# An identity matrix from VectorE and one small matmul, and GpSimd's constants in another order

## The chip, the cores and the metric

The kernel runs on one core of one Trainium2 chip. The metric is the device time in microseconds (us) of one execution. Its work is spread over the core's engines: TensorE (PE, with its weight loads shown apart as PEld), VectorE (DVE), ScalarE (ACT), GpSimd (POOL) and SyncE (SP), which here only issues DMAs. Each engine runs its own instructions in a fixed order; between engines they wait on semaphores that count finished instructions.

## What is computed

A parallel transformer block over 2048 positions of width 512: a layer norm, then a dilated local attention with 32 heads of 16 (8 keys for each query, two positions apart) and a gated GELU network of width 1376, both added to the input.

```python
x = A_x
xn = _layernorm(x, axis=-1)
return x + _A_ref(xn, A_wqkv, A_wo) + _B_ref(xn, B_w_gate, B_w_up, B_w_down)
```

In `_A_ref` the logits are dot products over 16 features with the keys at distances 0, 2, ... 14; positions before the start are masked; softmax over the 8 keys, a weighted sum of values, and a projection by `wo`. In `_B_ref` it is `gelu(xn @ w_gate) * (xn @ w_up) @ w_down`.

## The kernel before

The 2048 positions are cut into 4 blocks of 512, each into 4 tiles of 128; a pair of tiles (256 positions) is loaded as one `XIN` buffer. The program builds a graph of named tasks, one instruction or a run of matmuls each, and the table `ORDER` states by hand, engine by engine, the order in which the tasks are issued. From the graph come the semaphore waits; nothing is reordered at run time.

**The start.** SP loads the first tiles of x. PE meanwhile runs dummy matmuls on a constant of ones (`warm0` to `warm14`, L637): nine of 512 columns and one of 128 ahead of the first transposes, five of 128 behind them. DVE and ACT normalise tile 0 (`bnst0` L717, `bnag0` L743, `sub0` L828, `sq0` on ACT L753, `rstd0` L806, `norm0a/b` L847). PE transposes the first tiles against the identity `ident` (`tpx`, `tpy`, L888 and L877, four matmuls for each pair). From the transposed `xnT` it makes Q, K and V.

**The constants.** GpSimd makes, in this order: ones in `cf`, `onef` (for ACT's first table load), the identity by a selection on `cf` (L600) and a copy to bf16 (`c_idb`, L603), zeros in front of V (L618), `eps`, `mhalf`; then `E8`, a 128x32 matrix with 4 entries in each column that sums products over groups of 4 partitions: a fill (L607), two selections (L608, L611) and a copy to fp16 (L614); zeros in front of K (L616); the mask of the first positions, a fill (L622) and a selection (L623); zeros in `UT` (L621). DVE's first task is `c_wdz` (L620), zeros in a corner of `Wd`. A selection (`affine_select`) keeps or replaces each element by its place; each reads and writes SBUF. `cf`, `E8f` and `mask` are edited in place, so their steps wait for each other.

**Block 0's attention.** ACT copies the four Q tiles of block 0 out of PSUM (`evq0_0` to `evq0_3`, L988). DVE then multiplies Q by the 8 shifted views of K in two large `tensor_tensor` instructions of 8192 elements on each partition (`pr0_0`, `pr0_1`, L1066) and adds the halves (`pa0`, L1078). PE sums the products with `E8` (`er0_3`: 16 matmuls at L1102 for another purpose, then 16 with `E8` at L1109). DVE adds the mask once (L1132); ACT copies the logits out (`lc0`, L1138); the softmax goes on in short DVE steps that start with the maximum (L1143). DVE's queue around it reads `norm4 pr0_0 pr0_1 pa0 rstd8 h0_1 h0_0 mask d1a_0`, the h tasks being the products of the gated network (L1279).

**The later norms.** For tiles 8 to 15 the statistics come from ACT, which would need a table switch for a square root; GpSimd takes it instead as a power of one half over two columns (`sq8`, `sq10`, `sq12`, `sq14`, L799). `ve8` on ACT (L795) hands the variance to `sq8`; `rstd8` on DVE (L770) inverts it, and `norm8` on ACT (L820) uses it, with block 0's `gelu0_5` and `lc0` queued behind it.

GpSimd's queue and DVE's first task in `ORDER`, and the order in which a task is made to follow another of another engine:

```python
"pool":
    "c_ones c_onef c_id c_vnpad c_idb c_eps c_mhalf c_e8a c_e8b c_e8c c_e8d c_ktpad c_mask0 c_mask1 c_utz "
    "sq8 sq10 sq12 sq14",

def order_after(t, pred):
    if pred is not t and pred not in t.deps:
        t.deps.add(pred)
        t.odeps.add(pred)
```

Of the kernel before, what the change touches and what calls it, by code (L numbers as in the profile page):

```python
# [96 lines left out]
class Graph:  # L97
# [251 lines left out]
    def report(self):  # L349
# [4 lines left out]
BF = mybir.dt.bfloat16  # L354
F32 = mybir.dt.float32
FP16 = mybir.dt.float16
ALU = mybir.AluOpType
# [5 lines left out]

ORDER = {
# [34 lines left out]
    "dve":  # L399
# [10 lines left out]
    "pool":  # L410
        "c_ones c_onef c_id c_vnpad c_idb c_eps c_mhalf c_e8a c_e8b c_e8c c_e8d c_ktpad c_mask0 c_mask1 c_utz "
# [28 lines left out]
def bass_parallel_sum__sliding_local_dilated__glu_gated_geglu__prompt_kernel(nc, A_x, A_wqkv, A_wo, B_x, B_w_gate, B_w_up, B_w_down, out, dbg=None, cfg=None):  # L440
# [27 lines left out]
    QSC = 2.0 ** -6  # L468
# [15 lines left out]
    with contextlib.ExitStack() as es:  # L484
        def sb(name, shape, dt):
            return es.enter_context(nc.sbuf_tensor(name, shape, dt))
# [5 lines left out]
        Wd = sb("Wd", [128, NJ, 512], BF)  # L492
# [1 line left out]
        xnT = sb("xnT", [128, NXT, 4, 512], BF)  # L494
        KT = sb("KT", [128, 2, 4, 528], BF)
        ident = sb("ident", [128, 128], BF)
        cf = sb("cf", [128, 128], F32)
        E8 = sb("E8", [128, 32], FP16)
        E8f = sb("E8f", [128, 32], F32)
        mask = sb("mask", [32, 2, 4, 16], F32)  # L500
        one_l = nc.const_aps.tensor(1.0, [128, 128], BF)
        one_r = nc.const_aps.tensor(1.0, [128, 512], BF)
# [33 lines left out]
        PS = es.enter_context(nc.psum_tensor("PS", [128, 4096], F32))  # L536
# [7 lines left out]
        G = Graph()  # L544
        P_ps = Pool("ps", 8, psum=True, quotas=QUOTAS)
# [22 lines left out]
        I_wd = Item("Wd")  # L568
        I_wo = Item("Wo")
        I_ident = Item("ident")  # L570
        I_cf = Item("cf")
        I_E8 = Item("E8")
        I_E8f = Item("E8f")
# [21 lines left out]
        PC = -1000  # L595
        I_htz = Item("htz")
        PC2 = cfg.get("PC2", 8)
        G.task("pool", "c_ones", 0.2, lambda e: e.memset(cf[:, :], 1.0), wr=[I_cf], prio=PC)
        G.task("pool", "c_onef", 0.1, lambda e: e.memset(onef[:, :], 1.0), wr=[I_onef], prio=PC)
        G.task("pool", "c_id", 0.3, lambda e: e.affine_select(  # L600
            out=cf[:, :], in_=cf[:, :], pattern=[[-1, 128]], compare_op=ALU.is_equal, fill=0.0, base=0,
            channel_multiplier=1), rd=[I_cf], wr=[I_cf], prio=PC)
        G.task("pool", "c_idb", 0.65, lambda e: e.tensor_copy(out=ident[:, :], in_=cf[:, :]),  # L603
               rd=[I_cf], wr=[I_ident], prio=PC)
        G.task("pool", "c_mhalf", 0.1, lambda e: e.memset(mhalf[:, :], 0.5), wr=[I_mhalf], prio=PC2)
        G.task("pool", "c_eps", 0.1, lambda e: e.memset(eps[:, :], 1e-5), wr=[I_eps], prio=PC)
        G.task("pool", "c_e8a", 0.1, lambda e: e.memset(E8f[:, :], 0.25 / QSC), wr=[I_E8f], prio=PC2)  # L607
        G.task("pool", "c_e8b", 0.25, lambda e: e.affine_select(  # L608
            out=E8f[:, :], in_=E8f[:, :], pattern=[[-4, 32]], compare_op=ALU.is_ge, fill=0.0, base=0,
            channel_multiplier=1), rd=[I_E8f], wr=[I_E8f], prio=PC2)  # L610
        G.task("pool", "c_e8c", 0.25, lambda e: e.affine_select(  # L611
            out=E8f[:, :], in_=E8f[:, :], pattern=[[4, 32]], compare_op=ALU.is_ge, fill=0.0, base=3,
            channel_multiplier=-1), rd=[I_E8f], wr=[I_E8f], prio=PC2)
        G.task("pool", "c_e8d", 0.25, lambda e: e.tensor_copy(out=E8[:, :], in_=E8f[:, :]),  # L614
               rd=[I_E8f], wr=[I_E8], prio=PC2)
        G.task("pool", "c_ktpad", 0.15, lambda e: e.memset(KT[:, KTI[0].slot, :, 0:16], 0.0), wr=[(KTI[0], "pad")],  # L616
               prio=PC2)
        G.task("pool", "c_vnpad", 0.15, lambda e: e.memset(VN[:, VNI[0].slot, :, 0:16], 0.0), wr=[(VNI[0], "pad")],  # L618
               prio=PC2)
        G.task("dve", "c_wdz", 0.25, lambda e: e.memset(Wd[0:32, 10, :], 0.0), wr=[(I_wd, 2)], prio=PC + 1)  # L620
        G.task("pool", "c_utz", 0.6, lambda e: e.memset(UT[0:32, :], 0.0), wr=[I_htz], prio=PC2 + 20)  # L621
        G.task("pool", "c_mask0", 0.2, lambda e: e.memset(mask[:, :, :, :], 0.0), wr=[I_mask], prio=PC2)  # L622
        G.task("pool", "c_mask1", 0.3, lambda e: e.affine_select(  # L623
            out=mask[:, :, :, :], in_=mask[:, :, :, :], pattern=[[8, 2], [2, 4], [1, 16]],
            compare_op=ALU.is_ge, fill=-1.0e9, base=-14, channel_multiplier=0),
            rd=[I_mask], wr=[I_mask], prio=PC2 + 10)
        G.task("act", "c_tbl", 1.3, lambda e: e.activation(
            out=onef[:, 1:2], in_=onef[:, 0:1], func=ACTF.Sqrt),
            rd=[(I_onef, 0)], wr=[(I_onef, 1)], prio=PC, table="sqrt")
# [14 lines left out]
        for i, nm in enumerate(("q", "k", "v")):  # L644
            def mk(i=i):
# [4 lines left out]
                         prio=(-958, -957.5, -898)[i], nbytes=(900 if i == 0 else 512) * 1024)  # L650
# [10 lines left out]
        for (i, src, c0, c1, o) in ((0, B_w_gate, 1280, 1376, 32), (1, B_w_up, 1280, 1312, 0),  # L661
                                    (2, B_w_up, 1312, 1376, 128)):
            def mk(src=src, c0=c0, c1=c1, o=o):
# [8 lines left out]
            wr=[(I_wd, 0)], prio=R_WD, nbytes=2000 * 1024)  # L672
# [5 lines left out]
                     wr=[I_wo], prio=R_WD + 2, nbytes=512 * 1024)  # L678
# [9 lines left out]
        for p in range(NP):  # L688
            b = p // 2
            base = LN_BASE[b] + (p % 2) * 10  # L690
# [3 lines left out]
            if p < 2:  # L694
                for t2 in range(2):
                    def mk_ld(t2=t2, p=p, it=it_x):
# [3 lines left out]
                                 prio=((-960, -959), (-957.8, -956.5))[p][t2], nbytes=128 * 1024)  # L700
            else:
                def mk_ld(p=p, it=it_x):
# [3 lines left out]
                             prio=(0, 0, -897.5, -897)[p] if p < 4 else -950 + p * 20, nbytes=256 * 1024)  # L706
# [6 lines left out]
            for t2 in range(2):  # L713
                t = 2 * p + t2
# [3 lines left out]
                if t == 1:  # L718
                    for (nm, dur, kw, rd, wr) in (
# [6 lines left out]
                        def mk_a(kw=kw, it=it_x):  # L726
                            return lambda e: e.activation(**dict(dict(in_=XIN[:, it.slot, 1, :]), **kw))
                        t_of[nm] = G.task("act", nm, dur, mk_a(), rd=rd + ([] if "in_" in kw else xp(it_x, p, 1)),
                                          wr=wr, prio=-300)
                    t_of["mean1"] = G.task("dve", "mean1", 0.1, lambda e: e.tensor_scalar(  # L730
                        out=mv[:, 1, 0:1], in0=sums[:, 0:1], scalar1=1.0 / D, scalar2=None, op0=ALU.mult),
                        rd=[(I_sums, 0)], wr=[(I_mv, 1)], prio=tp0(t))
# [12 lines left out]
            for ts in (((2 * p,), (2 * p + 1,)) if b == 0 else ((2 * p, 2 * p + 1),)):  # L745
                t, n = ts[0], len(ts)
# [8 lines left out]
                if t < NSQA:  # L755
                    t_of["sq%d" % t] = G.task("act", "sq%d" % t, 0.15, mk_sa(), rd=[(I_sums, 2) if t == 1 else (I_mv, t), I_eps],
                                              wr=[(I_sq, t)], prio=pr - 100, table="sqrt")
                else:
# [12 lines left out]
                    if p < PACT:  # L771
                        t_of["sq%d" % t] = G.task(
                            "act", "sq%d" % t, 0.25, lambda e, t=t, n=n: e.activation(
                                out=sq[:, t:t + n], in_=mv[:, t:t + n, 1], func=ACTF.Sqrt, bias=eps[:, 0:1]),
                            rd=[(I_mv, q) for q in ts] + [I_eps], wr=[(I_sq, q) for q in ts], table="sqrt")
# [4 lines left out]
                    for t2 in range(2):  # L780
                        def mk_sqa(t=t + t2, t2=t2, it=it_x):
# [3 lines left out]
                               wr=[I_xs, (I_s2, t + t2)], prio=pr + 2)  # L785
                    small("act", "va", [I_s2], I_vb, scale(vb, s2, 1.0 / D))
                    if p < PPOW:
                        t_of["sq%d" % t] = G.task(
                            "act", "sq%d" % t, 0.25, lambda e, t=t, n=n: e.activation(
                                out=sq[:, t:t + n], in_=vb[:, t:t + n], func=ACTF.Sqrt, bias=eps[:, 0:1]),  # L790
                            rd=[(I_vb, q) for q in ts] + [I_eps], wr=[(I_sq, q) for q in ts], table="sqrt")
# [4 lines left out]
                            out=ve[:, t:t + n], in_=vb[:, t:t + n], func=ACTF.Identity, bias=eps[:, 0:1]),  # L796
                        rd=[(I_vb, q) for q in ts] + [I_eps], wr=[(I_ve, q) for q in ts])
# [11 lines left out]
            for t2 in range(2):  # L809
                t = 2 * p + t2  # L810
# [591 lines left out]
        for b in range(NB):  # L1402
            for j in range(NJ - 1):
                G.order_after(t_of["fu%d_%d" % (b, j)], t_of["fg%d_%d" % (b, j)])
                if j >= 4:
                    G.order_after(t_of["fg%d_%d" % (b, j)], t_of["fu%d_%d" % (b, j - 4)])
                if j >= 1:
                    G.order_after(t_of["fg%d_%d" % (b, j)], t_of["fg%d_%d" % (b, j - 1)])
                    G.order_after(t_of["fu%d_%d" % (b, j)], t_of["fu%d_%d" % (b, j - 1)])
        G.schedule(ORDER)  # L1410
        G.assign_sync(cnt, dsems)
        REPORT.update(G.report())
# [32 lines left out]
```

## Time and profile before

| what | value |
|---|---|
| time, median of 3 runs (lowest to highest) | 181.36 us (181.31 to 181.4) |
| time of the profiled execution | 181.5 us |
| span of its instructions | 180.0 us |
| mean traffic of the DMAs | 109 GB/s |
| HBM read and written | 14.71 MB, 3.15 MB |

The span runs from the first instruction of the program in the trace to the last; the 1.5 us between it and the time of the same execution lie around it. Rows of the timeline read: start in us from the span's begin, duration in us, engine, line of the kernel, operation, what it writes and reads, shape, count of merged instructions, and in brackets the engine's idle time before it with what ended it. The duration of one row of several instructions runs from the first start to the last end.

### The profile page before, as it was taken

The numbers are of one execution on the slowest core, as the hardware profiler recorded it, in microseconds if no ns is written. First come the engines' busy times: TensorE is split into PE (matmuls) and PEld (weight loads), VectorE is DVE, ScalarE is ACT, GpSimd is POOL, SyncE is SP. The second block draws the span as 40 slices with busy tenths as digits, with TensorE's granted clock in tenths as the row PEclk, the third lists the DMA queues.
The fourth block names the chain that finished last, engine by engine and source line by source line (L and its number), as shares of the span: only waits on it lengthen the run. The fifth ranks groups of instructions, "written<-read, shape, count | busy, mean of one in ns | idle before, by whom it ended". The sixth has DMA issues, their size and how long they took to land.

```text
span 180.0 us, 2755 instructions
## 1 busy us (share of the span) xinstructions
PE 176.1 (98%) x1043; PEld 91.7 (51%) x1060; DVE 168.8 (94%) x157; ACT 132.9 (74%) x270; POOL 20.0 (11%) x23
## 2 busy tenths in 40 slices
PE   8999999999999999999999999999999999999995
PEld 2897554444544445444444454444444444446555
DVE  3899998799999999999999999999999999999973
ACT  5689999999999998999895798953276676611111
POOL 6000160000720009207000000000000000000000
PEclk9999999999999999999999999999999999999999
DMA  4995690863260400002744000243060226810023
GB/s 125 362 357 152 121 324 13 293 224 98 58 227 18 98 4 0 0 0 60 193 129 88 29 0 0 77 123 124 18 217 4 58 58 192 272 60 4 0 73 102
DMA packets 27276, 19.60 MB, mean 109 GB/s; under 512 B 13856, under 2 KB 25088, under 8 KB 27264
## 3 DMA queue, kind: packets, MB, share of 16 engines
q1 hardware_dynamic: 27264, 19.44, 36.5%
q8 instruction: 8, 0.13, 0.3%
q14 instruction: 4, 0.03, 0.1%
HBM read 14.71 MB, written 3.15 MB: 99 GB/s over the span
## 4 chain that ended last, share of the span: by engine, by line
PE 96%; ACT 2%; issue 1%; DVE 0%
PE PS L1255 38%; PE PS L1347 29%; PE PS L1035 17%; PE PS L952 3%; PE PS L637 3%; PE PS L1010 2%; PE PS L1294 2%; PE PS L966 1%; PE PS L1102 1%; ACT UU L1272 1%; PE PS L1109 0%; PE PS L888 0%; ACT XS L736 0%; ACT XIN L820 0%; ACT OB L1380 0%
## 5 line engine op out<-in xcount | busy, mean ns | idle before, releaser
L1347 PE MATMUL PS<-Wd,HT 128*128 128x512 bf16 (+2 forms) x206 | 40.2, 345 | 0.2
L1255 PE MATMUL PS<-xnT,Wu 128*128 128x512 bf16 x158 | 39.0, 379 | 0.2 <-ACT UU L1272 0.2
L1255 PE MATMUL PS<-xnT,Wg 128*128 128x512 bf16 x155 | 38.4, 379 | 0.4 <-issue 0.2
L1217 DVE TENSOR_TENSOR UNI<-VN,PT 128x8192 f16<-128x8192 bf16 x8 | 35.2, 4416 | 0.0
L1066 DVE TENSOR_TENSOR UNI<-QT,KT 128x8192 f16<-128x8192 bf16 x8 | 35.2, 4417 | 0.0
L1035 PE MATMUL PS<-xnT,Wqkv 128*128 128x512 bf16 x140 | 34.0, 379 | 0.3 <-ACT XS L736 0.2
L1347 PEld LDWEIGHTS PS<-Wd,HT 128*128 128x128 bf16 x209 | 19.6, 98 | 19.0
L1380 ACT ACTIVATE OB<-PS 128x512 bf16<-128x512 f32 x14 | 8.3, 594 | 24.0 <-PE PS L1347 22.5
L1272 ACT ACTIVATE UU<-PS 128x512 bf16<-128x512 f32 x40 | 23.4, 605 | 3.0 <-PE PS L1255 1.5
L1265 ACT ACTIVATE GG<-PS 128x512 bf16<-128x512 f32 x40 | 23.2, 599 | 3.2 <-PE PS L1255 2.7
L1255 PEld LDWEIGHTS PS<-xnT,Wu 128*128 128x128 bf16 x160 | 15.5, 98 | 18.9 <-ACT GG L1265 0.4
L1255 PEld LDWEIGHTS PS<-xnT,Wg 128*128 128x128 bf16 x160 | 15.6, 98 | 18.5 <-ACT UU L1272 0.4
L799 POOL TENSOR_TENSOR sq<-ve,mhalf 128x2 bf16<-128x2 f32 x4 | 17.1, 4280 | 64.3 <-ACT ve L795 64.3
L1035 PEld LDWEIGHTS PS<-xnT,Wqkv 128*128 128x128 bf16 x144 | 16.2, 113 | 15.3 <-ACT GG L1265 0.4
L1078 DVE TENSOR_TENSOR UNI<-UNI 128x8192 f16<-128x8192 f16 x4 | 17.7, 4418 | 0.1
L1226 DVE TENSOR_TENSOR UNI<-UNI 128x8192 f16<-128x8192 f16 x4 | 17.7, 4419 | 0.0
L1347 PE MATMUL PS<-Wo,OT 128*128 128x512 bf16 (+2 forms) x74 | 16.0, 345 | 0.1
L1279 DVE TENSOR_TENSOR HT<-GG,UU 128x1024 bf16<-128x1024 bf16 x20 | 13.2, 684 | 0.4 <-ACT UU L1272 0.4
L1347 PEld LDWEIGHTS PS<-Wo,OT 128*128 128x128 bf16 x76 | 7.1, 98 | 6.5 <-DVE OT L1237 0.2
L1232 DVE TENSOR_TENSOR UNI<-UNI 128x4096 f16<-128x4096 f16 x4 | 9.1, 2287 | 0.1
L1046 ACT ACTIVATE VN<-PS 128x512 bf16<-128x512 f32 x12 | 7.1, 601 | 2.0 <-PE PS L1035 1.9
L1046 ACT ACTIVATE KT<-PS 128x512 bf16<-128x512 f32 x12 | 7.1, 602 | 1.6 <-PE PS L1035 1.5
(98 smaller groups left out, 181.1 us busy)
## 6 DMA issues: line engine op xcount, KB each, us to landing
PT<-pt_scratch SPq DMA_DIRECT2D x16, 256.0 KB, 4.0
out_dram<-OB SPq DMA_DIRECT2D x14, 128.0 KB, 2.1
XIN<-in_A_x_dram SPq DMA_DIRECT2D x12, 128.0 KB, 3.9
Wqkv<-in_A_wqkv_dram SPq DMA_DIRECT2D x3, 512.0 KB, 5.0
XIN<-in_A_x_dram SPq DMA_DIRECT2D x6, 256.0 KB, 5.3
Wg<-in_B_w_gate_dram SPq DMA_DIRECT2D x2, 640.0 KB, 6.6
Wu<-in_B_w_up_dram SPq DMA_DIRECT2D x2, 640.0 KB, 6.6
Wd<-in_B_w_down_dram SPq DMA_DIRECT2D x1, 1280.0 KB, 6.5
```

Of the source, the lines that this page charges most:

```text
L799: "pool", "sq%d" % t, 5.0, lambda e, t=t, n=n: e.tensor_tensor(out=sq[:, t:t + n], in0=ve[:, t:t + n], in1=mhalf[:, 0:n], op=ALU.pow),
L1035: ins = e.matmul(PS[:, 512 * it.slot:512 * it.slot + 512], lhsT=wcols(which, kt, g), rhs=xnT[:, itx.slot, kt, :], start=(kt == 0), stop=(k ...
L1046: return e.activation(out=o, in_=PS[:, 512 * it.slot:512 * it.slot + 512], func=ACTF.Identity, scale=(QSC, 1.0, 1.0)[which])
L1066: return lambda e: e.tensor_tensor(out=UNI[:, it.slot:it.slot + 2, :, :], in0=bass.AP(QT, (itq.slot * 4 + 2 * h) * 512, [[NQT * 4 * 512, 1 ...
L1078: return lambda e: e.tensor_tensor(out=UNI[:, i0.slot:i0.slot + 2, :, :], in0=UNI[:, i0.slot:i0.slot + 2, :, :], in1=UNI[:, i1.slot:i1.slo ...
L1217: return lambda e: e.tensor_tensor(out=bass.AP(UNI, ito.slot * 4096, [[NUNI * 4096, 128], [2048, 4], [512, 4], [1, 512]]), in0=bass.AP(VN, ...
L1226: return lambda e: e.tensor_tensor(out=UNI[:, i0.slot:i0.slot + 2, :, :], in0=UNI[:, i0.slot:i0.slot + 2, :, :], in1=UNI[:, i1.slot:i1.slo ...
L1255: ins = e.matmul(PS[0:M, 512 * it.slot:512 * it.slot + 512], lhsT=Wx[:, kt, j * 128:j * 128 + M], rhs=xnT[:, itx.slot, kt, :], start=(kt = ...
L1265: return lambda e: e.activation(out=GG[:, ito.slot, q, :], in_=PS[:, 512 * it.slot:512 * it.slot + 512], func=ACTF.Gelu_apprx_tanh)
L1272: return lambda e: e.activation(out=UU[:, ito.slot, q, :], in_=PS[:, 512 * it.slot:512 * it.slot + 512], func=ACTF.Identity)
L1279: return lambda e: e.tensor_tensor(out=HT[:, ito.slot, j - 1:j + 1, :], in0=GG[:, ig.slot, :, :], in1=UU[:, iu.slot, :, :], op=ALU.mult)
L1347: ins = e.matmul(PS[:, 512 * it.slot:512 * it.slot + CW], lhsT=(OT[:, ito.slot, q, ti * 128:(ti + 1) * 128] if kind == "o" else HT[:, ith. ...
```

## The change

The identity no longer comes from GpSimd. DVE writes the ramp 0, 1, ... 127 into `cf` (now bf16) on every partition by a prefix sum over ones (`c_ramp`); PE multiplies the ramp by a column of ones (`c_ix`, one column wide, between `warm1` and `warm2`), which gives 128 times the partition's own number in one column of a PSUM bank; DVE compares 128 times the ramp with that column (`c_id`) and so writes `ident`. GpSimd's fill of `cf`, its selection and its copy for the identity are gone. `c_wdz` moves from DVE to GpSimd. GpSimd's remaining fills come first; `E8`'s chain and the mask's selection come behind them, and `c_e8a`, the first of the chain, is made to follow `evq0_3`, block 0's last Q copy on ACT. `sq8` keeps its place at the queue's end.

```diff
     "pe":
-        "warm0 warm1 warm2 warm3 ...
+        "warm0 warm1 c_ix warm2 warm3 ...
     "dve":
-        "c_wdz bnst0 bnag0 sub0 ...
+        "c_ramp c_id bnst0 bnag0 sub0 ...
     "pool":
-        "c_ones c_onef c_id c_vnpad c_idb c_eps c_mhalf c_e8a c_e8b c_e8c c_e8d c_ktpad c_mask0 c_mask1 c_utz "
+        "c_onef c_vnpad c_eps c_mhalf c_ktpad c_mask0 c_utz c_wdz c_e8a c_e8b c_e8c c_e8d c_mask1 "
         "sq8 sq10 sq12 sq14",
...
-        cf = sb("cf", [128, 128], F32)
+        cf = sb("cf", [128, 128], BF)
...
-        G.task("pool", "c_ones", 0.2, lambda e: e.memset(cf[:, :], 1.0), wr=[I_cf], prio=PC)
+        it_ix = Item("cix", P_ps, "warm")
+        G.task("dve", "c_ramp", 0.3, lambda e: e.tensor_tensor_scan(
+            out=cf[:, :], data0=one_l, data1=one_l, initial=-1.0, op0=ALU.mult, op1=ALU.add), wr=[I_cf], prio=PC)
+        G.task("pe", "c_ix", 0.06, lambda e: e.matmul(
+            PS[:, 512 * it_ix.slot:512 * it_ix.slot + 1], lhsT=cf[:, :], rhs=one_r[:, 0:1], start=True, stop=True),
+            rd=[I_cf], wr=[it_ix], prio=PC, mode="f")
...
-        G.task("pool", "c_id", 0.3, lambda e: e.affine_select(
-            out=cf[:, :], in_=cf[:, :], pattern=[[-1, 128]], compare_op=ALU.is_equal, fill=0.0, base=0,
-            channel_multiplier=1), rd=[I_cf], wr=[I_cf], prio=PC)
-        G.task("pool", "c_idb", 0.65, lambda e: e.tensor_copy(out=ident[:, :], in_=cf[:, :]),
-               rd=[I_cf], wr=[I_ident], prio=PC)
+        G.task("dve", "c_id", 0.25, lambda e: e.tensor_scalar(
+            out=ident[:, :], in0=cf[:, :], scalar1=128.0, scalar2=PS[:, 512 * it_ix.slot:512 * it_ix.slot + 1],
+            op0=ALU.mult, op1=ALU.is_equal), rd=[I_cf, it_ix], wr=[I_ident], prio=PC)
...
-        G.task("dve", "c_wdz", 0.25, lambda e: e.memset(Wd[0:32, 10, :], 0.0), wr=[(I_wd, 2)], prio=PC + 1)
+        G.task("pool", "c_wdz", 0.6, lambda e: e.memset(Wd[0:32, 10, :], 0.0), wr=[(I_wd, 2)], prio=PC + 1)
...
+        G.order_after(t_e8a, next(t for t in G.tasks if t.name == "evq0_3"))
```

GpSimd's queue of before, from `E8`'s fill to the powers (line, operation, what it writes and reads, shape; a bracket names the engine whose count it waits for, `cnt_pool` being its own):

```order
L607 MEMSET E8f 128x32
L608 AFFINE_SELECT E8f<-E8f 128x32 [waits cnt_pool]
L611 AFFINE_SELECT E8f<-E8f 128x32 [waits cnt_pool]
L614 CAST E<-E8f 128x32 [waits cnt_pool]
L616 MEMSET KT 128x4x16
L622 MEMSET mask 32x128
L623 AFFINE_SELECT mask<-mask 32x128 [waits cnt_pool]
L621 MEMSET UT 32x512
L799 TENSOR_TENSOR sq<-ve,mhalf 128x2 [waits cnt_act] x4
```

The same stretch of the queue of the changed kernel (its lines lie up to three further down):

```order
L619 MEMSET KT 128x4x16
L625 MEMSET mask 32x128
L624 MEMSET UT 32x512
L623 MEMSET Wd 32x512
L610 MEMSET E8f 128x32 [waits cnt_act]
L611 ISA
L611 AFFINE_SELECT E8f<-E8f 128x32 [waits cnt_pool]
L614 AFFINE_SELECT E8f<-E8f 128x32 [waits cnt_pool]
L617 CAST E<-E8f 128x32 [waits cnt_pool]
L626 AFFINE_SELECT mask<-mask 32x128
L802 TENSOR_TENSOR sq<-ve,mhalf 128x2 [waits cnt_act] x4
```

The five steps from `E8`'s fill to the mask's selection now stand behind a wait for ACT, and directly in front of the powers. [...]

PE's first rows before:

```order
L637 MATMUL PS<-const-bfloat16-1.0 128x512 x9
L637 MATMUL PS<-const-bfloat16-1.0 128x128
L888 MATMUL PS<-ident,XIN 128x128 x4
L637 MATMUL PS<-const-bfloat16-1.0 128x128 x5
L966 MATMUL PS<-xnT,Wqkv 128x128 x8
```

and in the changed kernel:

```order
L640 MATMUL PS<-const-bfloat16-1.0 128x512 x2
L601 MATMUL PS<-const-bfloat16-1.0,cf 128x1
L640 MATMUL PS<-const-bfloat16-1.0 128x512 x7
L640 MATMUL PS<-const-bfloat16-1.0 128x128
L891 MATMUL PS<-ident,XIN 128x128 x4
```

One matmul of one column, with the ramp as its weights, stands behind the second dummy matmul. Behind it the order of PE, and the orders of ACT and SP throughout, are the same in both kernels; on DVE, `c_ramp` and `c_id` stand where `c_wdz` stood. `c_ix` takes one more PSUM bank in the rotation, so later tiles lie in other banks than before.

More of the change, by code (lines that the diff above doesn't have):

```diff
@@ L597, in bass_parallel_sum__sliding_local_dilated__glu_gated_geglu__prompt_kernel @@
         PC2 = cfg.get("PC2", 8)
-        G.task("pool", "c_ones", 0.2, lambda e: e.memset(cf[:, :], 1.0), wr=[I_cf], prio=PC)
-        G.task("pool", "c_onef", 0.1, lambda e: e.memset(onef[:, :], 1.0), wr=[I_onef], prio=PC)
-        G.task("pool", "c_id", 0.3, lambda e: e.affine_select(
-            out=cf[:, :], in_=cf[:, :], pattern=[[-1, 128]], compare_op=ALU.is_equal, fill=0.0, base=0,
-            channel_multiplier=1), rd=[I_cf], wr=[I_cf], prio=PC)
-        G.task("pool", "c_idb", 0.65, lambda e: e.tensor_copy(out=ident[:, :], in_=cf[:, :]),
-               rd=[I_cf], wr=[I_ident], prio=PC)
+        it_ix = Item("cix", P_ps, "warm")
[4 more added lines that the diff above has]
+            rd=[I_cf], wr=[it_ix], prio=PC, mode="f")
+        G.task("pool", "c_onef", 0.1, lambda e: e.memset(onef[:, :], 1.0), wr=[I_onef], prio=PC)
+        G.task("dve", "c_id", 0.25, lambda e: e.tensor_scalar(
+            out=ident[:, :], in0=cf[:, :], scalar1=128.0, scalar2=PS[:, 512 * it_ix.slot:512 * it_ix.slot + 1],
+            op0=ALU.mult, op1=ALU.is_equal), rd=[I_cf, it_ix], wr=[I_ident], prio=PC)
         G.task("pool", "c_mhalf", 0.1, lambda e: e.memset(mhalf[:, :], 0.5), wr=[I_mhalf], prio=PC2)
         G.task("pool", "c_eps", 0.1, lambda e: e.memset(eps[:, :], 1e-5), wr=[I_eps], prio=PC)
-        G.task("pool", "c_e8a", 0.1, lambda e: e.memset(E8f[:, :], 0.25 / QSC), wr=[I_E8f], prio=PC2)
+        t_e8a = G.task("pool", "c_e8a", 0.1, lambda e: e.memset(E8f[:, :], 0.25 / QSC), wr=[I_E8f], prio=PC2)
         G.task("pool", "c_e8b", 0.25, lambda e: e.affine_select(
```

4 rows, old and new, of the table ORDER are left out of this document.

## The prediction

> **What bounds the kernel now.** I read the page's first part, then the chain of work that ended last, then the timeline of the start, and last the stretch from 15 to 33 us, where the moved work lands.
>
> ```profile
> PE 176.1 (98%) x1043; PEld 91.7 (51%) x1060; DVE 168.8 (94%) x157; ACT 132.9 (74%) x270; POOL 20.0 (11%) x23
> PE 96%; ACT 2%; issue 1%; DVE 0%
> ```
>
> PE is busy for 98% of the span and is 96% of the chain, so a gain must shorten PE's stream or start it earlier. DVE at 94% is nearly as full: a delay that reaches DVE has little idle time to vanish in. POOL is idle almost throughout, and matters only where somebody waits for it.
>
> The start, from the timeline:
>
> ```profile
> 0.84 4.11 PE L637 MATMUL PS<-const-bfloat16-1.0 128*128 128x512 bf16 x10 [0.84 <-PEq L1430]
> 0.91 0.27 DVE L620 MEMSET Wd<- 32x256 uint32 x1 [0.91 <-PEq L1430]
> 3.78 0.15 PEld L637 LDWEIGHTS PS<-const-bfloat16-1.0 128*128 128x128 bf16 x1 [0.28 <-issue]
> 4.20 0.15 PEld L637 LDWEIGHTS PS<-const-bfloat16-1.0 128*128 128x128 bf16 x1 [0.28 <-issue]
> 1.43 0.29 POOL L603 CAST ident<-cf 128x128 bf16<-128x128 f32 x1
> 2.91 0.69 DVE L717 BATCH_NORM_STATS2 st<-XIN 128x6 f32<-128x512 bf16 x1 [1.73 <-DMA XIN<-in_A_x_dram]
> 4.92 0.34 PEld L888 LDWEIGHTS PS<-ident,XIN 128*128 128x128 bf16 x4 [0.57 <-DVE XIN L847]
> ```
>
> The identity is ready at 1.43 + 0.29 = 1.72 us and first used at 4.92. The first transpose waits for DVE's normalised tile, and DVE for the load of x until 2.91. Making the identity earlier or elsewhere therefore brings nothing by itself.
>
> **The change part by part. The start: 0.** DVE idles for 1.73 us before 2.91, so dropping `c_wdz` (0.27) gains nothing, and `c_ramp` and `c_id` have room. No prefix sum stands in the trace. On 128 columns I bound it, like `c_id`, by the 0.27 of the fill of 256 columns and the 0.69 of the statistics over 512. `c_ix` can run after two dummy matmuls, whose loads follow each other by 4.20 - 3.78 = 0.42, so at 0.84 + 0.84 = 1.68, or when the ramp is there, at the latest 0.91 + 0.69 = 1.60. With one more matmul's time for `c_ix`,
>
> ```profile
> L637 PE MATMUL PS<-const-bfloat16-1.0 128*128 128x128 bf16 x6 | 1.1, 314 | 0.0
> ```
>
> `c_id` starts at about 2.0 and ends at 2.3 to 2.7: before the load lands. If it ended behind 2.91, everything from `bnst0` on would move by the excess. On PE, `c_ix` and the reload of the ones push the dummies back. I take 0.1 for one column; a whole slot of 0.42 is the other end. PE's weight loads stood idle for 0.57 us before the first transpose, 0.42 of which the last wide dummy took, so 0.15 is spare: 0.1 is covered, 0.42 would cost 0.27. I take 0 and keep 0.3 for the range. GpSimd's fills, one 0.5 longer by `c_wdz`, end near 3 us; nothing waits for them.
>
> **The moved chain.** What it takes alone, with the fill that heads it:
>
> ```profile
> 1.72 0.12 POOL L607 MEMSET E8f<- 128x32 f32 x1
> 1.92 0.21 POOL L608 TENSOR_SCALAR_AFFINE_SELECT E8f<-E8f 128x32 f32<-128x32 f32 x1
> 2.19 0.21 POOL L611 TENSOR_SCALAR_AFFINE_SELECT E8f<-E8f 128x32 f32<-128x32 f32 x1
> 2.47 0.21 POOL L614 CAST E<-E8f 128x32 f16<-128x32 f32 x1
> 3.04 0.33 POOL L623 TENSOR_SCALAR_AFFINE_SELECT mask<-mask 32x128 f32<-32x128 f32 x1
> 3.32 0.51 POOL L621 MEMSET UT<- 32x512 bf16 x1
> ```
>
> Start to start that is 0.20, 0.27, 0.28 and, from the mask's selection to the next, 0.28. It now begins behind `evq0_3`:
>
> ```profile
> 15.22 0.60 ACT L988 ACTIVATE QT<-PS 128x512 bf16<-128x512 f32 x1
> 16.04 8.76 DVE L1066 TENSOR_TENSOR UNI<-QT,KT 128x8192 f16<-128x8192 bf16 x2
> 24.82 4.42 DVE L1078 TENSOR_TENSOR UNI<-UNI 128x8192 f16<-128x8192 f16 x1
> 29.17 0.16 DVE L770 RECIPROCAL rstd<-sq 128x2 f32<-128x2 bf16 x1
> 29.57 0.71 ACT L820 ACTIVATE XIN<-XIN,rstd 128x512 bf16<-128x512 bf16 x1
> 29.84 0.62 PE L1102 MATMUL PS<-xnT,Wt 128*32 128x256 bf16 x16
> ```
>
> `evq0_3` ends at 15.82; with 0.09 for the handover (`ve8` below ends at 21.66, `sq8` starts at 21.75) the fill starts at 15.91, the first selection at 16.11. From 16.04 to 29.24 DVE runs three instructions of 4.4 us without a break, each with two inputs in SBUF. Alone the chain would end at 17.3, far ahead of `sq8`. But look at how long the powers take beside such instructions:
>
> ```profile
> 21.37 0.29 ACT L795 ACTIVATE ve<-vb,eps 128x2 f32<-128x2 bf16 x1
> 21.75 3.61 POOL L799 TENSOR_TENSOR sq<-ve,mhalf 128x2 bf16<-128x2 f32 x1 [17.91 <-ACT ve L795]
> 45.83 4.43 DVE L1078 TENSOR_TENSOR UNI<-UNI 128x8192 f16<-128x8192 f16 x1
> 46.25 4.57 POOL L799 TENSOR_TENSOR sq<-ve,mhalf 128x2 bf16<-128x2 f32 x1 [20.89 <-ACT ve L795]
> 64.06 4.42 DVE L1226 TENSOR_TENSOR UNI<-UNI 128x8192 f16<-128x8192 f16 x1
> 69.73 0.68 DVE L1279 TENSOR_TENSOR HT<-GG,UU 128x1024 bf16<-128x1024 bf16 x1
> 70.33 2.28 DVE L1232 TENSOR_TENSOR UNI<-UNI 128x4096 f16<-128x4096 f16 x1
> 67.65 5.51 POOL L799 TENSOR_TENSOR sq<-ve,mhalf 128x2 bf16<-128x2 f32 x1 [16.84 <-ACT ve L795]
> 80.25 4.42 DVE L1066 TENSOR_TENSOR UNI<-QT,KT 128x8192 f16<-128x8192 bf16 x1
> 81.78 3.43 POOL L799 TENSOR_TENSOR sq<-ve,mhalf 128x2 bf16<-128x2 f32 x1 [8.62 <-ACT ve L795]
> ```
>
> The powers end at 25.36, 50.82, 73.16 and 85.21. The DVE instructions beside them end at 24.80 (the second of the pair at L1066), 50.26, 72.61 and 84.67: 0.54 to 0.56 earlier in all four cases, though the powers' durations differ by 2 us. So **GpSimd's instruction is held until DVE's large one is over**. I take the same for each selection and the copy, which read and write SBUF too. Then one step gets through at each end: the first selection at 20.4, the second at 24.8, the copy at 29.24. Behind it DVE stands still, because `rstd8` needs `sq8` and `sq8` is last in GpSimd's queue; from here the steps run unhindered. The copy ends at 29.24 + 0.21 = 29.45, the mask's selection takes 0.28, so `sq8` starts at 29.73.
>
> What `sq8` takes alone no row shows. It lies between 0.54 (the part behind DVE's end) and 3.43 (the shortest row, which may hold some waiting). I take 3.43, because of the third row: it was already running when a 4.4-us instruction ended at 68.48, and it let that end and the ends of short ones up to 70.41 go by, as if it wasn't yet ready to use them. Own work of 2.76 us or more (70.41 less 67.65) and 2.89 or less (84.67 less 81.78), then a held end, fits all four rows. `sq8` then ends at 33.16 and `rstd8` starts at 33.25 instead of 29.17, 4.1 late.
>
> **What that costs.** ACT's `norm8` could have started at 29.42 (29.33 and a handover); now it can at 33.5, so 3.9 behind its 29.57. Everything behind it on ACT waits too, `lc0` among it, and DVE's softmax behind `lc0`:
>
> ```profile
> 32.87 0.42 DVE L1143 TENSOR_TENSOR SU<-PB 128x512 bf16<-128x512 bf16 x1 [1.21 <-ACT PB L1138]
> 29.20:33.00 3.80, 3.62 (x43) 1.74 (x42) 1.84 (x6) 3.75 (x8) 0.00 (x0) 1.00 0.25 71
> 33.00:152.00 119.00, 118.21 (x603) 56.12 (x613) 118.44 (x87) 98.67 (x195) 13.51 (x3) 1.00 0.30 87
> PEld PS L1347 <- DVE OT L1237: 0.2, 1, 0.2
> ```
>
> In the two windows the columns after the length are PE, PEld, DVE, ACT. ACT is busy for 3.75 of 3.80 us, so `lc0` and DVE's L1143 come 3.85 late. From 33 to 152 us DVE is busy for 118.44 of 119 and can win back at most 0.56; I take 0.3, since part of that idle time waits for ACT, which is late too. At the end of that stretch PE's output matmuls wait for DVE's attention result (the last row), so what DVE has lost by then PE has lost: 3.85 - 0.3, or **3.5 us**. PE itself won't stop at 29 us: its next matmuls need only earlier copies. It loses the time piecemeal where its PSUM banks wait for ACT and for DVE. `er0_3` (29.84) finds `E8` ready since 29.45 and is not late; the mask is wanted later still.
>
> Sum against the profiled execution: 181.5 + 0 + 3.5 = 185.0. It lies 0.14 above the median of the runs, so for them 184.9.
>
> **The rivals.** *The power is short.* The Trainium skill, page "SBUF — State Buffer", section "Who interferes with whom", says that a VectorE instruction with two SBUF inputs contends with a GpSimd instruction that reads SBUF, and that whichever issued first has the shared ports for the whole instruction while the other blocks fully. By that rule all of `sq8` but 0.54 was waiting; the first, second and fourth rows agree, while the third should have ended near 69.0 and ended at 73.16. From the rows: with 0.54 alone, `sq8` ends at 30.27 and `rstd8` starts at 30.36, 1.2 late; less 0.15 on ACT and 0.35 as above leaves 0.7, so 182.1. A power of some 1.5 us gives 183.
>
> *The selections are not held, or two pass in one gap.* Only two-input powers are seen held here, no selection is. If the chain is over by about 25.7 (29.17 less 3.43 and 0.09), `rstd8` is on time, DVE and ACT run as before and the time is 181.4: no change. That is the rival on the other side, and the point of decision is the end of the mask's selection. Against it stands that only one hold fits ahead of that point with all four steps done.
>
> *Nothing passes until DVE stops.* Then all four steps run from 29.24: the copy ends at 30.0, `sq8` starts at 30.28, and the time is 185.4. `E8` would then be just late for `er0_3`.
>
> **How the numbers follow.** The forecast (held, long power) has 0.57; held with a shorter power 0.22; not held 0.15; the start gaining a little 0.03; something dearer 0.03. The range goes from 182.0, the short power, to 185.9, which adds 0.5 for steps that miss a gap and 0.3 for `c_ix`; it leaves out the not-held case and the tails, about 0.2. A measurement of this kernel can tell about 0.2% (0.36 us) from no change. Slower by more than that: 0.81; within it: 0.16; faster: 0.03.
>
> **What would show it.** In the changed profile the two selections and the copy should end just behind 20.4, 24.8 and 29.24, `sq8` should start at 29.7 and take 3.4 us with no DVE instruction beside it, and DVE should idle for 4 us before `rstd8`, with POOL as what ended it. `bnst0` should still wait for the load until 2.9 and the first transpose start at 4.9 to 5.0. I am wrong if the mask's selection ends before 25 us, or if `sq8` alone takes well under 3 us.

## The result and the profile after

| | before | changed |
|---|---|---|
| median of 6 runs (lowest to highest) | 181.41 us (181.31 to 181.56) | 182.50 us (182.17 to 183.00) |
| profiled execution, its span | 181.5, 180.0 us | 182.68, 181.1 us |

The ratio is 1.0061 with an interval of 1.0044 to 1.0078: the change makes the kernel slower by 0.6%, or 1.1 us. The prediction was 184.9; its direction was right and its size was three times too large.

The page of the changed kernel, its first part and the engines of the chain that ended last:

```profile
PE 177.6 (98%) x1061; PEld 91.0 (50%) x1061; DVE 169.2 (93%) x158; ACT 132.8 (73%) x270; POOL 31.9 (18%) x21
...
PE 77%; ACT 10%; POOL 8%; DMA 3%; issue 1%; SPq 0%; DVE 0%; POOLq 0%
```

POOL has 11.9 us more of busy time from two instructions fewer, and it has come onto the chain: 8%, where before it was not named. What it does there stands in its timeline (start, duration, engine, line, operation; lines after the start of the program are 3 higher than before):

```profile
16.10 0.30 POOL L610 MEMSET E8f<- 128x32 f32 x1 [13.92 <-ACT QT L991]
16.48 8.60 POOL L611 TENSOR_SCALAR_AFFINE_SELECT E8f<-E8f 128x32 f32<-128x32 f32 x1
25.15 4.39 POOL L614 TENSOR_SCALAR_AFFINE_SELECT E8f<-E8f 128x32 f32<-128x32 f32 x1
29.60 0.21 POOL L617 CAST E<-E8f 128x32 f16<-128x32 f32 x1
29.75 0.33 POOL L626 TENSOR_SCALAR_AFFINE_SELECT mask<-mask 32x128 f32<-32x128 f32 x1
30.06 0.68 POOL L802 TENSOR_TENSOR sq<-ve,mhalf 128x2 bf16<-128x2 f32 x1
```

Two selections that took 0.21 us each at the start of the old kernel now take 8.60 and 4.39. They end at 25.08 and 29.54, each less than 0.1 us behind the end of a large DVE instruction (16.25 + 8.75 = 25.00 and 25.04 + 4.42 = 29.46 in the next fence). The row ISA, which the changed queue has between the fill and the first selection, shows no time of its own: from the fill's end to the selection's start it is 0.08 us (16.40 to 16.48), as in the kernel before, which has no such row there (1.84 to 1.92). Behind them, with DVE still, the copy, the mask's selection and the power run at their own speed, and **the power takes 0.68 us**.

DVE's timeline around it, then ACT's `norm8` from ACT's:

```profile
16.25 8.75 DVE L1069 TENSOR_TENSOR UNI<-QT,KT 128x8192 f16<-128x8192 bf16 x2
25.04 4.42 DVE L1081 TENSOR_TENSOR UNI<-UNI 128x8192 f16<-128x8192 f16 x1
30.78 0.17 DVE L773 RECIPROCAL rstd<-sq 128x2 f32<-128x2 bf16 x1 [1.31 <-POOL sq L802]
...
34.28 0.43 DVE L1146 TENSOR_TENSOR SU<-PB 128x512 bf16<-128x512 bf16 x1 [1.95 <-ACT PB L1141]
...
30.98 0.72 ACT L823 ACTIVATE XIN<-XIN,rstd 128x512 bf16<-128x512 bf16 x1 [1.08 <-DVE rstd L773]
```

`rstd8` starts at 30.78 instead of 29.17, `norm8` 1.41 later than before, the softmax at L1146 also 1.41 later. PE itself stops much later. Its weight loads' waits between 30 and 49 us (what waits, what ended the wait, us in total, times, longest):

```profile
PEld PS L1258 <- ACT GG L1268: 1.6, 3, 0.8
```

They wait for ACT's gelu, which reads its input from PSUM and so frees a bank, near 44, 45 and 47 us. Set side by side with before, PE's instructions are 0.2 us late until 42 us, 1.0 late from 45 us on, and 1.1 late at the end.

### The profile page after: what moved, and what is told of

The parts are those of the page before. It is cut to its first block, busy times and chain, and to the rows that moved or that the text cites. A ratio compares the mean times of both kernels' runs of the same rounds, so it can differ in the third digit from the quotient of the medians.

```text
span 181.1 us, 2774 instructions
## 1 busy us (share of the span) xinstructions
PE 177.6 (98%) x1061; PEld 91.0 (50%) x1061; DVE 169.2 (93%) x158; ACT 132.8 (73%) x270; POOL 31.9 (18%) x21
## 4 chain that ended last, share of the span: by engine, by line
PE 77%; ACT 10%; POOL 8%; DMA 3%; issue 1%; SPq 0%; DVE 0%; POOLq 0%
PE PS L1350 29%; PE PS L1258 28%; PE PS L1038 13%; POOL E8f L611 5%; DMA Wqkv<-in_A_wqkv_dram 3%; POOL E8f L614 2%; PE PS L955 1%; PE PS L1297 1%; ACT XS L739 1%; PE PS L969 1%; PE PS L1105 1%; ACT GG L1268 1%; ACT UT L1313 1%; PE PS L1112 1%; ACT L1268 1%; ACT L1163 1%
## 5 line engine op out<-in xcount | busy, mean ns | idle before, releaser
L1258 PE MATMUL PS<-xnT,Wu 128*128 128x512 bf16 x160 | 39.5, 379 | 0.4 <-ACT GG L1268 0.3
L1258 PE MATMUL PS<-xnT,Wg 128*128 128x512 bf16 x160 | 38.9, 379 | 0.0
L1268 ACT ACTIVATE GG<-PS 128x512 bf16<-128x512 f32 x40 | 23.7, 612 | 3.1 <-PE PS L1258 2.7
L802 POOL TENSOR_TENSOR sq<-ve,mhalf 128x2 bf16<-128x2 f32 x4 | 16.5, 4136 | 39.8 <-ACT ve L798 39.8
L611 POOL TENSOR_SCALAR_AFFINE_SELECT E8f<-E8f 128x32 f32<-128x32 f32 x1 | 8.6, 8603 | 0.1
```

What stands on the lines that cost most here:

```text
L611: G.task("pool", "c_e8b", 0.25, lambda e: e.affine_select(out=E8f[:, :], in_=E8f[:, :], pattern=[[-4, 32]], compare_op=ALU.is_ge, fill=0.0 ...
L802: "pool", "sq%d" % t, 5.0, lambda e, t=t, n=n: e.tensor_tensor(out=sq[:, t:t + n], in0=ve[:, t:t + n], in1=mhalf[:, 0:n], op=ALU.pow),
L1258: ins = e.matmul(PS[0:M, 512 * it.slot:512 * it.slot + 512], lhsT=Wx[:, kt, j * 128:j * 128 + M], rhs=xnT[:, itx.slot, kt, :], start=(kt = ...
L1268: return lambda e: e.activation(out=GG[:, ito.slot, q, :], in_=PS[:, 512 * it.slot:512 * it.slot + 512], func=ACTF.Gelu_apprx_tanh)
```

## Which part costs it: e1 and e2

The theory was that all of the loss comes through `sq8`; the rival was that a part of it comes from the start, since in the profiled run the load of `Wqkv` lands later. One kernel has the new identity with the chain left at the start, the other the old identity with the chain moved.

```diff
(e1_identity_alone, against the changed kernel)
-        G.order_after(t_e8a, next(t for t in G.tasks if t.name == "evq0_3"))
(e2_chain_alone, against the kernel before)
-        ... c_mhalf c_e8a c_e8b c_e8c c_e8d c_ktpad c_mask0 c_mask1 c_utz "
+        ... c_mhalf c_ktpad c_mask0 c_utz c_e8a c_e8b c_e8c c_e8d c_mask1 "
+        G.order_after(next(t for t in G.tasks if t.name == "c_e8a"),
+                      next(t for t in G.tasks if t.name == "evq0_3"))
```

> The new identity without the moved chain: the four E8 steps and the mask selection follow the fills at the start, as before. Theory (all of the loss comes through sq8): the chain is over by about 4 us, sq8 starts at about 21.8 as before, rstd8 at about 29.2 to 29.4, and the time is that of before, 181.3 to 181.7. Rival (the start costs: in the profiled run of after the Wqkv load lands about 0.5 us later, and DVE begins the first large product at 16.25 in place of 16.04): 0.2 to 0.5 us stay with the identity, 181.7 to 182.0, and rstd8 is late by the same 0.2.

> The identity stays on GpSimd as before; only the E8 steps and the mask selection move behind evq0_3. Theory: the first selection is held through two large products, the second through the sum, copy, mask selection and power (about 0.7 us) run after 29.3, rstd8 starts at about 30.6, 1.4 us late, and the time is 182.2 to 182.6. Rival (the start costs): 181.4 to 181.8, with rstd8 as late as that or later.

e1 took 181.57 us beside 181.53 for the kernel before on the same chip: ratio 1.0002 (0.9990 to 1.0014). e2 took 182.56: 1.0043 (1.0027 to 1.0058). **The identity costs nothing, the moved chain all that can be measured.** POOL's and DVE's timelines, first of e1, then of e2:

```profile
21.58 3.60 POOL L802 TENSOR_TENSOR sq<-ve,mhalf 128x2 bf16<-128x2 f32 x1 [18.18 <-ACT ve L798]
...
29.00 0.15 DVE L773 RECIPROCAL rstd<-sq 128x2 f32<-128x2 bf16 x1
```

```profile
16.44 8.61 POOL L608 TENSOR_SCALAR_AFFINE_SELECT E8f<-E8f 128x32 f32<-128x32 f32 x1
...
30.03 0.70 POOL L799 TENSOR_TENSOR sq<-ve,mhalf 128x2 bf16<-128x2 f32 x1
...
30.76 0.17 DVE L770 RECIPROCAL rstd<-sq 128x2 f32<-128x2 bf16 x1 [1.33 <-POOL sq L799]
```

The late landing of `Wqkv` is not the identity's doing either. Its first matmuls, in the timelines of PE of the changed kernel and of e2, which has the old identity:

```profile
6.44 0.64 PE L969 MATMUL PS<-xnT,Wqkv 128*128 128x128 bf16 x8 [0.35 <-DMA Wqkv<-in_A_wqkv_dram]
```

```profile
6.40 0.64 PE L966 MATMUL PS<-xnT,Wqkv 128*128 128x128 bf16 x8 [0.68 <-DMA Wqkv<-in_A_wqkv_dram]
```

In e1, which has the new one, they start at 5.87, as in the kernel before (5.89), and in e5 below, which has both the new identity and the moved chain, at 5.81. So this varies from run to run, and the 0.2 us by which all of DVE was late at 16 us in the profiled run are of that kind: the first large product starts between 15.73 and 16.25 in the profiles of the kernels with the new identity, and at 16.04 and 16.22 in the two with the old.

## What a late power costs: e3

Seven fills ahead of `sq8` put `rstd8` near the place where the prediction had it (33.87 against 33.25).

```diff
...
+        for i in range(7):
+            G.task("pool", "c_f%d" % i, 0.45, lambda e: e.memset(spare[:, :], 0.0), wr=[I_spare], prio=PC2 + 30)
...
-        "... c_mask1 "
+        "... c_mask1 c_f0 c_f1 c_f2 c_f3 c_f4 c_f5 c_f6 "
         "sq8 ...
```

> The changed kernel with seven GpSimd fills of a spare buffer (about 0.45 us each, 3 us in all) ahead of sq8, which puts rstd8 near 33.8, where the prediction had it with a power of 3.4 us. Theory (each us by which rstd8 is late behind about 29.7 costs one of the whole): 185.2 to 185.8. Rival (PE has reserves, and only a part of the delay reaches the end): 183.0 to 184.5.

It took 185.84 us, ratio 1.0233 (1.0215 to 1.0251). POOL's and DVE's timeline, then PE's waits between 30 and 49 us:

```profile
29.59 3.59 POOL L633 MEMSET spare<- 128x440 bf16 x7
33.14 0.69 POOL L806 TENSOR_TENSOR sq<-ve,mhalf 128x2 bf16<-128x2 f32 x1
...
33.87 0.17 DVE L777 RECIPROCAL rstd<-sq 128x2 f32<-128x2 bf16 x1 [4.86 <-POOL sq L806]
```

```profile
PEld PS L1262 <- ACT GG L1272: 1.9, 2, 1.2
PEld PS L1262 <- ACT PB L1145: 1.5, 1, 1.5
```

PE waits for the same gelus (L1272 here) and for `lc0` (L1145), 1.5 us for that one alone. `rstd8` is 4.70 us later than in the profile of before and the span 4.2 longer (184.2 to 180.0). In the changed kernel it is 1.61 later and the span 1.1 longer. From the one to the other both grow by 3.1: behind the first 0.5 us, which vanish, each microsecond of delay costs one. All profiles bear this out. In the nine kernels where `rstd8` is late (the changed one, e2, e3, e5 to e7 and e9 to e11, with starts from 30.18 to 33.87) the span ends 150.3 us behind the start of `rstd8`, each time; in the four where it is on time (before, e1, e4, e8) it ends 150.8 to 151.0 behind it. The prediction had the delay at 4.1 and the cost at 3.5, so the size of its last step holds.

## Where the chain may stand: e4 and e8

```diff
(e4_power_first, against the changed kernel)
-        "... c_utz c_wdz c_e8a c_e8b c_e8c c_e8d c_mask1 "
-        "sq8 sq10 ...
+        "... c_utz c_wdz "
+        "sq8 c_e8a c_e8b c_e8c c_e8d c_mask1 sq10 ...
(e8_chain_earlier, against the changed kernel)
-        G.order_after(t_e8a, next(t for t in G.tasks if t.name == "evq0_3"))
+        G.order_after(t_e8a, next(t for t in G.tasks if t.name == "evk0_1"))
```

> The changed kernel with sq8 ahead of the E8 steps in GpSimd's order. Theory: sq8 issues at about 21.8, ends about 0.55 after DVE's second product at about 25.5, rstd8 runs right behind the sum at about 29.3; the two selections go through behind the sum, E8 is there at about 30.1, before its first reader on PE at 30.3 to 30.5, and the time is 181.3 to 181.7. Rival (E8 or the mask comes too late for PE's and DVE's readers, or a selection is held by the short products behind the sum): PE's L1112 waits, 182 to 183.

> The changed kernel with the chain behind ScalarE's second K copy (evk0_1, near 11.7) in place of the last Q copy (near 15.9). Theory (the loss comes only from the large instructions that VectorE runs from 16 us on): each step gets through between VectorE's short instructions, the chain is over by about 14 to 15 us, rstd8 starts at about 29.2 to 29.4, and the time is 181.3 to 181.8. Rival (VectorE's short instructions follow without gaps and hold the selections too): the chain drags on past 16, the rest of it is held like in the changed kernel, and the time lies near 182.

e4 took 181.74 us, ratio 1.0019 (0.9999 to 1.0040); e8 took 181.38 beside 181.39, ratio 1.0010 (0.9994 to 1.0025). Both take the loss away, and neither beats the kernel before. POOL's timeline of e8, and its last step in e4:

```profile
11.88 0.13 POOL L610 MEMSET E8f<- 128x32 f32 x1 [9.70 <-ACT KT L991]
12.08 0.21 POOL L611 TENSOR_SCALAR_AFFINE_SELECT E8f<-E8f 128x32 f32<-128x32 f32 x1
...
12.80 0.33 POOL L626 TENSOR_SCALAR_AFFINE_SELECT mask<-mask 32x128 f32<-32x128 f32 x1
21.90 3.61 POOL L802 TENSOR_TENSOR sq<-ve,mhalf 128x2 bf16<-128x2 f32 x1 [8.77 <-ACT ve L798]
```

```profile
29.75 0.80 POOL L626 TENSOR_SCALAR_AFFINE_SELECT mask<-mask 32x128 f32<-32x128 f32 x1
...
29.65 1.41 DVE L1282 TENSOR_TENSOR HT<-GG,UU 128x1024 bf16<-128x1024 bf16 x2 [0.39 <-ACT UU L1275]
```

Four microseconds earlier, beside DVE's statistics, which have one input, each step takes what it takes alone. In e4 the mask's selection meets two 16-bit products: it takes 0.80 instead of 0.33, and the pair of products 1.41 instead of 1.29. Some of e4's small excess, if it is one, may come from there: its profile ends 151.0 us behind `rstd8`, the other three on time 150.8 to 150.9. That was not tested.

## What lets GpSimd through: e5, e6, e7, e9, e10, e11

The prediction had the first selection through at the end of the first product, near 20.4; it was held over that end. In each of these kernels one thing changes at that end: what DVE issues next.

```diff
+                if b == 0 and h == 0:       (a new "gap0" between pr0_0 and pr0_1 in DVE's order)
+  e5:  e.tensor_copy(out=spare[:, 0:2], in_=UNI[:, it.slot + 1, 7, 510:512])   rd=[pr_items[0]]
+  e6:  e.reciprocal(out=spare[:, 0:2], in_=mhalf[:, 0:2])
+  e9:  e.tensor_tensor(out=spare[:, 0:2], in0=mhalf[:, 0:2], in1=mhalf[:, 0:2], op=ALU.mult)
+  e10: e.tensor_tensor(out=spare[:, :], in0=Wqkv[:, 0, 0:440], in1=Wqkv[:, 1, 0:440], op=ALU.mult)
+  e11: as e10, and byn["gap0"].waits.append((cnt["act"], byn["evq0_3"].val))
(e7: no new instruction)
+        byn["pr0_1"].waits.append((cnt["act"], byn["evq0_3"].val))
```

> The changed kernel with a tiny VectorE copy between the two large products of block 0; it reads the last two columns that the first product wrote, so it must wait for that product's end, and VectorE's stream has a gap there, as it has ahead of the sum. Theory (GpSimd's reads get through only where VectorE's next instruction does not overlap the end of the last): the first selection ends about 0.07 us after the first product, near 20.7, the second behind the second product near 25.2, the copy goes through behind the sum near 29.7, and sq8 starts within 0.2 us of 30.1 as in the changed kernel; the time stays within 0.3 us of 182.5. Rival (the first selection has to sit out two products whatever stands between): it ends near 25.2 again.

> The changed kernel with a tiny VectorE reciprocal (2 columns of a constant) between the two large products of block 0; it depends on nothing there, so the stream should run on without a gap. Theory (a gap is needed): the first selection is held through both products and ends near 25.2, as in the changed kernel. Rival (what counts is what VectorE issues next: a small one-input instruction lets GpSimd in, as rstd8 behind the sum did for a selection in the run with the power first): it ends near 20.8.

> The changed kernel, only that the second large product of block 0 carries a wait on ScalarE's count, one that was met long before (evq0_3). Rival rule (the ends at which the power went through without a gap, 50.3 and 84.7 in the profile of before, were followed by an instruction that waits on another engine's semaphore, and this lets GpSimd in): the first selection ends near 20.7. If the wait counts for nothing: near 25.2, as in the changed kernel. The time within 0.3 us of 182.5 either way.

> The changed kernel with a tiny float32 VectorE product (2 columns of a constant, two inputs) between the two large products of block 0, with nothing to wait for. If any two-input instruction that overlaps the end keeps GpSimd out: the first selection ends near 25.2, as in the changed kernel. If only the 16-bit products at two elements a cycle do, as the large ones are: it ends within 0.1 us of the first product's end, near 20.4 to 20.7, as behind the reciprocal. The time stays within 0.3 us of 182.4.

> The changed kernel with a bf16 VectorE product of 440 columns (two inputs, about 0.37 us) between the two large products of block 0, with nothing to wait for. If 16-bit two-input products that overlap the end keep GpSimd out: the first selection ends near 25.6. If what counts is that the same instruction follows itself: near 20.7. The time within 0.5 us of 182.6.

> As the last, and the 440-column product also waits on ScalarE's count (met long before), like the two products behind which the power went through without a gap (L1279 at 50.3 and L1385 at 84.7 in the profile of before). If a 16-bit product with such a wait lets GpSimd in: the first selection ends near 20.7 while it ends near 25.6 in the run without the wait. If the wait counts for nothing: both end alike.

| run | between the products | first selection's end, from the first product's end | time, one run |
|---|---|---|---|
| changed kernel | nothing | 4.4 us | |
| e7 | nothing, second product waits on ACT (met) | 4.4 us | 182.37 |
| e10 | bf16 product, 440 columns | 4.7 us | 182.75 |
| e11 | the same with a wait on ACT (met) | 4.7 us | 182.60 |
| e9 | float32 product, 2 columns | 0.09 us | 182.13 |
| e6 | reciprocal, 2 columns | 0.07 us | 182.17 |
| e5 | copy that reads the product | 0.07 us | 182.13 |

The ends are counted from the first product's end because the whole stretch starts up to 0.5 us earlier or later from run to run. The kernel before took 181.4 beside them. The contrast in two timelines, first e6, then e10:

```profile
15.93 4.42 DVE L1070 TENSOR_TENSOR UNI<-QT,KT 128x8192 f16<-128x8192 bf16 x1
20.26 0.16 DVE L1081 RECIPROCAL spare<-mhalf 128x2 f32<-128x2 f32 x1
...
16.15 4.27 POOL L612 TENSOR_SCALAR_AFFINE_SELECT E8f<-E8f 128x32 f32<-128x32 f32 x1
```

```profile
15.95 4.42 DVE L1070 TENSOR_TENSOR UNI<-QT,KT 128x8192 f16<-128x8192 bf16 x1
20.28 0.38 DVE L1081 TENSOR_TENSOR spare<-Wqkv 128x440 bf16<-128x440 bf16 x1
20.58 4.42 DVE L1070 TENSOR_TENSOR UNI<-QT,KT 128x8192 f16<-128x8192 bf16 x1
...
16.17 8.90 POOL L612 TENSOR_SCALAR_AFFINE_SELECT E8f<-E8f 128x32 f32<-128x32 f32 x1
```

In both, the inserted instruction starts less than 0.1 us before the product ends (20.26 and 20.28 against 20.35 and 20.37), so my theory that a gap is needed fell with e6. At this end, what DVE issues next decides: behind the tiny reciprocal, the tiny float32 product and the copy that has to wait, the selection gets in; a 16-bit product that overlaps the end keeps it out, with 8192 columns or 440, and a wait on it that is met changes nothing. In e5, e6 and e9 the copy is held through the sum in its turn and ends just behind it. e5's `sq8` starts at 29.47 and not within 0.2 us of 30.1, mostly because its first product starts 0.52 us earlier than the changed kernel's. Type and length are not separated at this end: no kernel had a 16-bit product of two columns or a long float32 one. At another end, at 69.88 us in the changed kernel, a bf16 step of 0.21 us (L1146), hardly longer than e9's 0.19, left GpSimd's third power outside.

**One thing stays open**: the second and fourth powers of the old kernel went through at 50.26 and 84.67, where 16-bit products overlap the end too:

```profile
50.18 1.28 DVE L1279 TENSOR_TENSOR HT<-GG,UU 128x1024 bf16<-128x1024 bf16 x2
...
84.58 0.42 DVE L1385 TENSOR_TENSOR OB<-OB,XR 128x512 bf16<-128x512 bf16 x1
```

What tells those two ends apart from e10's is not shown.

## Why the prediction was wrong in size

*The start, 0.* Right: e1. The prefix sum took 0.42 us, between the bounds of 0.27 and 0.69, and `ident` was ready at 1.92 + 0.32 = 2.24, ahead of the load of x. DVE's timeline of the changed kernel, then PE's weight load of the first transpose, 0.03 later than before:

```profile
0.83 0.42 DVE L599 TENSOR_TENSOR_SCAN cf<-const-bfloat16-1.0 128x128 bf16<-128x128 bf16 x1 [0.83 <-PEq L1434]
1.92 0.32 DVE L605 TENSOR_SCALAR ident<-cf,PS 128x128 bf16<-128x128 bf16 x1 [0.67 <-PE PS L601]
2.96 0.69 DVE L720 BATCH_NORM_STATS2 st<-XIN 128x6 f32<-128x512 bf16 x1 [0.73 <-DMA XIN<-in_A_x_dram]
...
4.95 0.34 PEld L891 LDWEIGHTS PS<-ident,XIN 128*128 128x128 bf16 x4 [0.57 <-DVE XIN L850]
```

*GpSimd's instructions are held while DVE's large ones run.* Right, and shown for selections (8.60 and 4.39 us instead of 0.21), which had no row before.

*One step through at each end: 20.4, 24.8, 29.24.* Wrong at the first end. It cost little: the copy, the only step that this pushes behind the sum, takes 0.21 there. From the first product's start, `sq8` starts 13.69 us later in the prediction, 13.81 in the changed kernel, and 13.65 in e9, where the steps do pass one at each end (and the inserted product makes DVE's stretch 0.1 longer). The rule of the Trainium skill, page "SBUF — State Buffer", section "Who interferes with whom", by which the loser blocks until the holder's instruction is over, would have let the first selection in at 20.7; the trace has it at 25.08, so an instruction's end is not enough.

***`sq8` alone takes 3.43*: the step that failed.** It takes 0.68 to 0.70 in the changed kernel, e2 and e3. (That the power alone takes well under 3 us was one of the prediction's own signs of being wrong.) The 3.43 was chosen for the third power of the old kernel, which let the ends from 68.48 to 70.41 go by, "as if it wasn't yet ready to use them". Since the work is 0.7 us, it was ready and was kept out. In the old kernel it ended 0.55 us behind 72.61, the first end since its start with a gap behind it, for DVE's next row starts at 72.70:

```profile
72.70 0.42 DVE L1169 TENSOR_TENSOR SU<-EX 128x512 f16<-128x512 f16 x1
```

The changed kernel's third power shows it again; POOL's row first, then DVE's:

```profile
68.63 7.61 POOL L802 TENSOR_TENSOR sq<-ve,mhalf 128x2 bf16<-128x2 f32 x1 [16.41 <-ACT ve L798]
...
71.74 2.28 DVE L1235 TENSOR_TENSOR UNI<-UNI 128x4096 f16<-128x4096 f16 x1
73.94 0.41 DVE L1172 TENSOR_TENSOR SU<-EX 128x512 f16<-128x512 f16 x1
74.28 1.21 DVE L1240 TENSOR_TENSOR OT<-UNI 128x2048 bf16<-128x2048 f16 x1
75.41 0.28 DVE L1172 TENSOR_TENSOR SU<-SU 128x256 f16<-128x256 f16 x1
75.73 0.29 DVE L1172 TENSOR_TENSOR ms<-SU 128x128 f32<-128x128 f16 x1
```

It lasts 7.61 us, which no work of 2.8 us and one hold of a 2.28-us instruction explains, and ends at 76.24, 0.55 behind 75.69: the end of the first row in this run of 16-bit instructions whose successor (75.73) does not overlap it. That the prediction's 2.76 to 2.89 us fitted all four rows was chance.

*What a delay costs.* Right in size: 4.1 late for 3.5 in the prediction, 1.61 for 1.1 and 4.70 for 4.2 measured. The way was right in part. That PE would lose the time piecemeal where its banks wait for ACT holds, but nearly all is lost there by 45 us, and not taken over from DVE at 152 us. DVE's last attention product before that point comes 1.24 us late (151.68 against 150.44, L1240 and L1237), so DVE won back 0.17 since its softmax (1.41 late) and not the 0.3 of the sum. What softened the delay is PE, which came 1.0 us late behind an ACT that was 1.4 late; that the sum's 0.3 stood about for this is luck.

With 0.68 in the place of 3.43 the delay shrinks by 2.75, and the sum of 3.5 becomes 0.75. The profiled run adds 0.21 for the late load and 0.12 for the first end: 1.1, which is what its span shows. The rival with the short power, held as well, had named the right cause: 182.1 us from 0.54.

## What to carry to other kernels

The duration of a row on GpSimd beside a busy VectorE is no price (here 3.4 to 7.6 us for 0.7 us of work): subtract the hold, or find a row of the same operation with VectorE still, before it enters a sum. A few small GpSimd steps in one queue ahead of a step that somebody waits for were cheap here only if they were over before VectorE's long stream of 16-bit two-input instructions began: four microseconds earlier, or behind the awaited step, made the 1.1 us of loss vanish. Where several rows of one operation differ, the odd one asks which of the others' conditions it lacked, before it is taken as the measure.

## What the runs showed that was not expected

A GpSimd selection of 32 columns can be kept out over several VectorE instructions in a row: 8.60 us over two products, 8.90 over three, and 7.61 for the power of two columns. Even a tiny VectorE instruction of another kind (0.16 us) at the seam between two products lets it in. VectorE may be held in its turn: in e4, beside the mask's selection of 0.80 us, its pair of products took 1.41 instead of 1.29, in one profile.
